# Retention in pairs of tiles, with states made a pair ahead, in a kernel of retention, routed experts and a dense layer

## Chip, core and metric

The kernel runs on one core of a Trainium2 chip. The metric is the device time of one execution in microseconds. Engines are called TensorE (PE in the rows; PEld is its loading of stationary operands), VectorE (DVE), ScalarE (ACT), GpSimd (POOL) and SyncE (SP, which issues most of the DMAs).

## What is computed

```python
def _attn_ref(q, k, v):                      # (8, 8, 576, 64) each
    scores = 1 / sqrt(64) * (q @ k.T)
    gamma = 1.0 - 2.0 ** (-5.0 - arange(8))
    Dmat = where(rel >= 0, gamma[:, None, None] ** rel, 0.0)   # rel: distance of two positions
    return (scores * Dmat) @ v

def _moe_ref(x, w_gate, w1, w2):             # x (4608, 512), 8 experts of 1024
    logits = x @ w_gate
    expert_idx = argmax(logits, axis=1)
    gate_w = softmax(logits)[arange(N), expert_idx]
    for e in range(E):
        mask = expert_idx == e
        out[mask] = gate_w[mask, None] * (maximum(x[mask] @ w1[e], 0.0) @ w2[e])

def _moe2_ref(x, w_in, w_out):               # 512 -> 2048 -> 512
    return maximum(x @ w_in, 0.0) ** 2 @ w_out
```

The output is `_moe2_ref` of `_moe_ref` of the retention, in float32.

## The kernel before

**Retention** (lines 327 to 705) treats 36 tiles of 128 tokens with all eight heads. A sequence of 576 tokens has four chunks of 128 and one of 64; the fifth chunks of two sequences share a tile (`kind` gives sequence and chunk, chunk 4 being such a tile). Per tile `t`: `scores` multiplies keys and queries (64 rows of the array, both halves at once) into two PSUM banks, and VectorE multiplies them with a causal mask (line 393). `scale_v` scales the values on GpSimd. `out_x` adds two products in one bank: the inner one, of the state that earlier chunks left and the queries (line 435, or line 428 for chunk 4, where queries spread out with zeros in `zq` keep the two sequences apart), and the outer one, of values and masked scores (line 439, two 64-wide halves of the array). VectorE scales the result (447) and transposes it in blocks (451); every second tile SyncE writes the rows of two to `x_d` (`put`, four DMAs). `state` adds keys times values to an accumulator in PSUM (line 411), from which ScalarE copies the state for the next chunk (418).

**Routing** runs along. After two tiles, `logits` multiplies the pair with the gate weights (line 472; 32 columns of the array), ScalarE copies the result, and a `fold` one tile later transposes it (481) and VectorE sums it. When a group of eight (or six) tiles has its logits, `group` makes six steps of it: `one` (VectorE, the largest logit), `two` (matmuls that count, line 522 on, and four vector operations), `three` (ranks, lines 558 to 229), `first` of `route` (hit and b, 238 and 242), `second` (matmuls, 249) and `third` (253 or 255). One step is taken per tile. Behind the third group, `lead_rows` fetches two tiles of tokens for the first expert, and `lead_turn` transposes each of them into a bank of the scores' pool (ScalarE 603, VectorE 604).

**Order.** Each engine executes its instructions in the order in which the program is written; nothing reorders them. The loop over `t` (644 to 693) issues the load of tile t + 4, the writes of the last pair, scores of t + 1, values of t + 2, the fold, logits, `out_x` and `state` of t, and one routing step. Input tiles have five buffers (a tile is 1 MB), scores three PSUM banks, results two, the accumulator, the logits and the routing one each. Four expert units are loaded at tiles 12, 18, 24 and 30 (`load_unit`) and split into a high and a low part two tiles later by ScalarE and GpSimd (`split_unit`).

Behind the loop the **experts** begin with the lead tiles (`first(0, (0,))`, line 955, whose first matmul reads the high part of both and whose second reads the low part), among which the last fold, routing steps and logits stand; experts and the **dense layer** (line 1144 on) fill the rest.

Of the kernel before, what the change touches and what calls it, by code (L numbers as in the profile page):

```python
# [19 lines left out]
NT = 36  # L20
# [33 lines left out]
def body(ctx, tc, att, tab_v, tab_x, masks, wg, ident, pick, cst, wu, wd, out):  # L54
# [269 lines left out]
    rt = scope(chain, "rt", 1, side="right")  # L324
    lg_ps = scope(chain, "lg_ps", 1, PSUM, side="right")
    rt_ps = scope(chain, "rt_ps", 1, PSUM, side="right")
    with ExitStack() as es:
# [5 lines left out]
        r_p = scope(es, "r_p", 2)  # L333
        sc_ps = scope(es, "sc_ps", 3, PSUM)
        x_ps = scope(es, "x_ps", 2, PSUM)
# [7 lines left out]
        lgt = rt.tile([128, NT, NE], F32, name="lgt")  # L343
        zq = tabs.tile([128, 4, 3, 64], F32, name="zq")
        sts = [tabs.tile([128, 4, 128], F32, name=f"sts{i}") for i in range(4)]

        in_t, vs_t, r_t, st_acc, xp_t, xr_t = {}, {}, {}, {}, {}, {}
        lead_s = []
# [8 lines left out]
        def load(t):  # L357
# [5 lines left out]
            else:  # L363
                sp.dma_start(out=a[:, 0:n], in_=att[t, :, 0:n])

        def spread_q(t):
            if kind(t)[1] == 4:
                q = in_t[t][:, 0].rearrange("p (h n) -> p h n", h=4)
                act.activation(out=zq[:, :, 0], in_=q[:, :, 0:64], func=AF.Copy)
                act.activation(out=zq[:, :, 2], in_=q[:, :, 64:128], func=AF.Copy)  # L370

# [47 lines left out]

        def out_x(t):  # L420
            b, c = kind(t)
            q = in_t[t][:, 0].rearrange("p (h n) -> p h n", h=4)
            ps = x_ps.tile([128, 4, 128], F32, tag="x", name="x")
            if c == 4:
                for i in range(2):
                    s = stslot(i, 3)
                    for p in range(4):
                        pe.matmul(
                            ps[:, p], s[:, p], zq[:, p, i:i + 2].rearrange("p a n -> p (a n)"),
                            start=(p == 0 and i == 0), stop=False, skip_group_check=True,  # L430
                        )
            elif c > 0:
                s = stslot(b, c - 1)
                for p in range(4):
                    pe.matmul(ps[:, p], s[:, p], q[:, p], start=(p == 0), stop=False, skip_group_check=True)  # L435
# [15 lines left out]
            vec.transpose(  # L451
                out=xr[:, 4 * (t % 2):4 * (t % 2) + 4].rearrange("q t k j -> q k t j"),
                in_=x.rearrange("q k (t i) -> q k t i", i=32),
            )
            if t % 2 == 0:
                return

            def put():
                rows = x_d[128 * t - 128:128 * t + 128, :].rearrange("(t i) (a c) -> a i t c", i=32, a=4)
                for a in range(4):  # L460
                    sp.dma_start(
                        out=rows[a], in_=xr[32 * a:32 * a + 32].rearrange("q t k j -> q t (k j)")
                    )

            late.append(put)

        def logits(j):
            x = xp_t.pop(j)
            both = lg_ps.tile([128, 2, 256], F32, tag="lg", name="lg")
            ps = both[:, 0]  # L470
# [18 lines left out]

        total = [None]  # L490

        def group(t0, t1):
# [143 lines left out]
        for a in sts:  # L636
            vec.memset(a, 0.0)
        vec.memset(zq, 0.0)
        vec.memset(wg2, 0.0)
        scale_v(0)  # L640
        scores(0)
        scale_v(1)
        fold = None
        for t in range(NT):
            ready, late[:] = late[:], []
            if t + 4 < NT:
                load(t + 4)
            if t == 0:
                sp.dma_start(out=wg2[:, :, 0:NE], in_=wg)
            if t == 2:  # L650
                sp.dma_start(out=idn, in_=ident)
            if t == 4:
# [4 lines left out]
            if t % 6 == 0 and 12 <= t < 36:  # L657
                raw[t] = load_unit(t // 6 - 2)
            if t + 1 < NT:
                scores(t + 1)  # L660
            if t + 2 < NT:
                scale_v(t + 2)
            if t == 1:
                vec.reciprocal(out=step, in_=tabx[:, 0, :, 0])
                vec.tensor_tensor(out=step, in0=step, in1=tabx[:, 1, :, 0], op=ALU.mult)
            if t in (1, 2):
                pool.tensor_tensor(
                    out=tabx[:, t + 1], in0=tabx[:, t], in1=step.unsqueeze(2).to_broadcast([128, 4, 128]), op=ALU.mult
                )
            if t == 4:  # L670
                for s in range(2):
# [3 lines left out]
                    )  # L675
            if fold:
                fold()
                for g in GROUPS:
                    if g[1] == t - 2:
                        todo += group(*g)  # L680
            fold = logits((t - 3) // 2) if t % 2 and t > 2 else None
            out_x(t)
            state(t)
            if t + 1 < NT:
                spread_q(t + 1)
            if NT - 1 - LEAD <= t < NT - 1:
                lead_turn(t - NT + 1 + LEAD)
            if todo and t < NT - 1:
                todo.pop(0)()
            if t == 8:  # L690
                vec.tensor_copy(ub, cf[:, C_U:C_U + 128])
            if t % 6 == 2 and 12 <= t < 36:
                split_unit(t // 6 - 2, raw.pop(t - 2), pool)()
        for f in late:
# [11 lines left out]


    xt_p = scope(ctx, "xt_p", 2, reuse="tile")
    HALF = CAP // 2
# [57 lines left out]
    with ExitStack() as es:  # L767
# [187 lines left out]
        first(0, (0,))  # L955
        fold()
        for f in todo:
# [565 lines left out]
```

## Time and profile before

| | us |
|---|---|
| median of 3 runs | 1352.97 (1352.24 to 1353.36) |
| the profiled execution | 1352.63 |
| its span | 1350.8 |
| TensorE busy | 1338.0 (99%) |
| VectorE, ScalarE, GpSimd busy | 835.2, 545.9, 256.6 |
| first expert matmul starts | 155.87 |

Busy time of TensorE counts a matmul from its start to its modelled end; several overlap, so it shows where TensorE had no work and not how fast it was. The retention is the first 155.87 us.

### The profile page before, as it was taken

How to read it: one execution, taken by the hardware profiler on the slowest of the kernel's cores; microseconds unless marked ns; L12 is line 12 of the kernel's file. 1: busy time of each engine (PE TensorE's matmuls, PEld its weight loads, DVE VectorE, ACT ScalarE, POOL GpSimd, SP SyncE). 2: the span in 40 equal slices, each digit the busy share in tenths (PEclk: the TensorE clock that was granted, in tenths of full speed). 3: DMA queues.
4: the chain of work that ended last, by engine and by line, in shares of the span. 5: the costliest groups of instructions: out<-in, count | busy, mean ns of one | idle time of the engine just before them, and what ended most of it. 6: DMA issues, size and time to landing. Idle time of an engine off the chain costs nothing.

```text
span 1350.8 us, 21535 instructions
## 1 busy us (share of the span) xinstructions
PE 1338.0 (99%) x8113; PEld 1152.5 (85%) x8113; DVE 835.2 (62%) x1512; ACT 545.9 (40%) x1064; POOL 256.6 (19%) x265
## 2 busy tenths in 40 slices
PE   8999999999999999999999999999999999999998
PEld 6888899999999999989888888888888888888887
DVE  6888858788788887636755563346624465245422
ACT  1232335445454553425544443345423454244321
POOL 3243263141332421112210030001300012000000
PEclk9999999999999999999999999999999999999999
DMA  9999678788978877567766666665766666565563
GB/s 341 344 350 323 175 225 291 256 299 262 299 256 255 301 257 268 202 243 269 284 232 203 208 218 233 216 223 195 251 210 225 212 221 235 201 215 194 190 230 110
DMA packets 129904, 328.32 MB, mean 243 GB/s; under 512 B 20350, under 2 KB 74110, under 8 KB 107776
## 3 DMA queue, kind: packets, MB, share of 16 engines
q1 hardware_dynamic: 121600, 305.72, 66.2%
q0 software_dynamic: 8192, 21.15, 5.3%
q8 instruction: 65, 1.06, 0.3%
q14 instruction: 47, 0.39, 0.1%
HBM read 266.10 MB, written 61.75 MB: 243 GB/s over the span
## 4 chain that ended last, share of the span: by engine, by line
PE 81%; issue 6%; DMA 6%; DVE 5%; ACT 2%; SPq 1%; POOL 0%; POOLq 0%; DVEq 0%; ACTq 0%
PE b L1187 25%; PE fa L1260 10%; PE fa L1259 10%; PE fa L1261 10%; PE l L830 3%; PE l L831 3%; PE l L832 3%; PE acc L854 3%; PE acc L855 3%; PE acc L856 3%; PE sc L387 2%; PE x L439 2%; PE x L435 1%; DMA in<-att 1%; PE stp L411 1%
## 5 line engine op out<-in xcount | busy, mean ns | idle before, releaser
L1187 PE MATMUL b<-xt,wq 128*128 128x512 f32 (+1 forms) x1296 | 265.2, 362 | 2.8 <-DMA wq<-ws_d 1.1
L1187 PEld LDWEIGHTS b<-xt,wq 128*128 128x128 f32 x1296 | 221.1, 188 | 41.9 <-DMA wq<-ws_d 1.5
L1259 PE MATMUL fa<-wq,ch 128*128 128x512 f32 x576 | 224.1, 389 | 0.0
L1260 PE MATMUL fa<-wq,ch 128*128 128x512 f32 x576 | 224.1, 389 | 0.0
L1261 PE MATMUL fa<-wq,cl 128*128 128x512 f32 x576 | 224.1, 389 | 0.0
L1249 DVE TENSOR_TENSOR cl<-g,ch 128x512 fp32r<-128x512 f32 (+1 forms) x160 | 108.6, 687 | 175.3 <-ACT ch L1248 172.9
L1248 ACT ACTIVATE ch<-g 128x512 fp32r<-128x512 f32 (+1 forms) x160 | 91.5, 584 | 183.5 <-PE fa L1260 183.5
L750 POOL TENSOR_TENSOR xsum<-yf 128x256 f32<-128x256 f32 x80 | 63.8, 805 | 452.8 <-DVE yf L738 389.1
L832 PE MATMUL l<-xt,w 128*128 128x320 f32 (+1 forms) x480 | 149.2, 311 | 0.0
L831 PE MATMUL l<-xt,w 128*128 128x320 f32 (+1 forms) x480 | 149.2, 311 | 0.0
L830 PE MATMUL l<-xt,w 128*128 128x320 f32 (+1 forms) x480 | 149.0, 310 | 0.1
L1261 PEld LDWEIGHTS fa<-wq,cl 128*128 128x128 f32 x576 | 108.1, 188 | 22.6 <-DVE cl L1249 0.2
L1259 PEld LDWEIGHTS fa<-wq,ch 128*128 128x128 f32 x576 | 108.1, 188 | 22.4
L1260 PEld LDWEIGHTS fa<-wq,ch 128*128 128x128 f32 x576 | 108.1, 188 | 22.4
L854 PE MATMUL acc<-w,hh 128*128 128x512 f32 x320 | 125.6, 393 | 0.1
L855 PE MATMUL acc<-w,hh 128*128 128x512 f32 x320 | 125.3, 392 | 0.0
L856 PE MATMUL acc<-w,hl 128*128 128x512 f32 x320 | 124.7, 390 | 0.0
L1173 ACT ACTIVATE s<-b 128x512 f32<-128x512 f32 (+1 forms) x120 | 66.5, 555 | 105.0 <-PE b L1187 105.0
L836 ACT ACTIVATE hh<-l 128x320 fp32r<-128x320 f32 (+2 forms) x128 | 54.4, 436 | 121.1 <-PE l L832 117.0
L1208 DVE TENSOR_TENSOR s<-s,s 128x512 f32<-128x512 f32 (+1 forms) x40 | 25.5, 638 | 113.7 <-ACT s L1173 113.7
L830 PEld LDWEIGHTS l<-xt,w 128*128 128x128 f32 x480 | 90.1, 188 | 2.6 <-DVE hl L837 0.4
L1187 PE MATMUL b<-xe,wq 128*128 128x512 f32 x384 | 92.2, 389 | 0.0
(181 smaller groups left out, 2082.0 us busy)
## 6 DMA issues: line engine op xcount, KB each, us to landing
wq<-ws_d SPq DMA_DIRECT2D x142, 1024.0 KB, 4.9
raw<-wu SPq DMA_DIRECT2D x62, 512.0 KB, 5.3
in<-att SPq DMA_DIRECT2D x28, 1024.0 KB, 8.1
craw<-wd SPq DMA_DIRECT2D x32, 512.0 KB, 5.2
ws_d<-cw SPq DMA_DIRECT2D x24, 512.0 KB, 4.4
x_d<-xr SPq DMA_DIRECT2D x72, 128.0 KB, 6.1
r_d<-row SPq DMA_DIRECT2D x35, 256.0 KB, 4.7
xs<-r_d SPq DMA_DIRECT2D x140, 64.0 KB, 4.4
```

Source lines behind the costliest of these rows:

```text
L830: pe.matmul(ps, w[:, 0, k], hi[:, k, cs], start=(k == 0), stop=False)
L831: pe.matmul(ps, w[:, 0, k], lo[:, k, cs], start=False, stop=False)
L832: pe.matmul(ps, w[:, 1, k], hi[:, k, cs], start=False, stop=(k == 3))
L854: pe.matmul(acc[i], hh[:, cs], w[:, 0], start=(f == 0), stop=False)
L855: pe.matmul(acc[i], hh[:, cs], w[:, 1], start=False, stop=False)
L856: pe.matmul(acc[i], hl[:, cs], w[:, 0], start=False, stop=(f == 7))
L1187: pe.matmul(ps, w[:, a, c], xc[T][i, b][c], start=(i in (5, 1, 4) and m == 0), stop=(m == 5), skip_group_check=True,)
L1248: act.activation(out=hi[:, o], in_=s, func=AF.Copy)
L1249: vec.tensor_tensor(out=lo[:, o], in0=s, in1=hi[:, o].bitcast(F32), op=ALU.subtract)
L1259: pe.matmul(acc[i], hi[:, cs], w[:, 0], start=(f == 0), stop=False)
L1260: pe.matmul(acc[i], hi[:, cs], w[:, 1], start=False, stop=False)
L1261: pe.matmul(acc[i], lo[:, cs], w[:, 0], start=False, stop=(f == 15))
```

## The change

The loop goes over pairs of tiles. In one pass it issues scores of both tiles, logits of the pair before, inner products of both, the fold, routing matmuls, and then for each tile its outer products, with the state of the second tile between them and the state of the next pair's first tile behind them. `out_x` falls into `inner` and `outer`. The transpose of a pair's second tile is issued in the next pass, behind the masks, with the writes that need it. Routing steps: at most one that begins with a matmul is taken per pass (the set `on_pe`), directly behind the fold, and then all up to the next such step. Scores have four banks, and the logits use one of them in turn; the logits' own bank is there only behind the loop. `zq` is gone: chunk 4's inner products take 64 query columns per sequence. Loads of t + 5 and t + 6 stand at the end of the pass; the gate weights and the identity are loaded in the first pass. Expert units are loaded from tile 24 on, one a pass, and split one pass later. The lead tiles are transposed at the end of the last two passes.

```diff
-        sc_ps = scope(es, "sc_ps", 3, PSUM)
+        sc_ps = scope(es, "sc_ps", 4, PSUM)
...
-        def out_x(t):
+        def inner(t):
...
                     for p in range(4):
+                        cs = slice(64 * i, 64 * i + 64)
                         pe.matmul(
-                            ps[:, p], s[:, p], zq[:, p, i:i + 2].rearrange("p a n -> p (a n)"),
+                            ps[:, p, cs], s[:, p], q[:, p, cs],
...
+        def outer(t):
+            b, c = kind(t)
+            ps = ps_t.pop(t)
...
-            late.append(put)
+            late.append(lambda: (spin(), put()))
...
-            both = lg_ps.tile([128, 2, 256], F32, tag="lg", name="lg")
+            if j < NT // 2 - 1:
+                both = sc_ps.tile([128, 4, 128], F32, tag="sc", name="lg").rearrange("p a b -> p (a b)")
...
+            on_pe.update((two, steps[4]))
...
-        for t in range(NT):
+        for t in range(0, NT, 2):
...
+            if t + 2 < NT:
+                scale_v(t + 2)
+            scores(t)
+            scores(t + 1)
             for f in ready:
                 f()
...
+            fold = logits(t // 2 - 1) if t else None
+            inner(t)
+            if t:
+                inner(t + 1)
+                fold()
+            if todo and todo[0] in on_pe:
+                todo.pop(0)()
+            for g in GROUPS:
+                if g[1] == t:
+                    todo += group(*g)
+            while todo and todo[0] not in on_pe:
+                todo.pop(0)()
+            outer(t)
+            if t == 0:
+                inner(1)
+            state(t + 1)
+            outer(t + 1)
+            if 2 < t + 2 < NT:
+                state(t + 2)
+            for u in (t + 5, t + 6):
+                if u < NT:
+                    load(u)
+            if t + 3 < NT:
+                scale_v(t + 3)
...
+            if t >= NT - 2 * LEAD:
+                lead_turn((t - NT) // 2 + LEAD)
+            if t == 24:
+                raw[0] = load_unit(0)
+            if 24 < t <= 32:
+                u = t // 2 - 13
+                split_unit(u, raw.pop(u), pool)()
+                if u < 3:
+                    raw[u + 1] = load_unit(u + 1)
```

TensorE, tiles 6 and 7 before: `sc` are scores, `lg<-x` logits, `lg<-idn` the fold, `x<-in` inner and `x<-r` outer products, `stp` states; of the outer products only the first row stands.

```order
L387 MATMUL sc<-in 128x128 x8
L472 MATMUL lg<-x,wg_144 32x256 x4
L435 MATMUL x<-in,sts_147 128x128 x4
L439 MATMUL x<-r_462,vs 64x128
...
L411 MATMUL stp<-vs,in 64x64 x8
L387 MATMUL sc<-in 128x128 x8
L481 MATMUL lg<-idn,ls 128x128 x2
```

The same engine after the change, a pass in which both tiles have an inner product:

```order
L379 MATMUL sc<-in 128x128 x16
L476 MATMUL lg<-x,wg_141 32x256 x4
L428 MATMUL x<-in,sts_144 128x128 x4
L428 MATMUL x<-in,sts_143 128x128 x4
L485 MATMUL lg<-idn,ls 128x128 x2
L436 MATMUL x<-r_507,vs 64x128
...
L403 MATMUL stp<-vs,in 64x64 x8
L436 MATMUL x<-r_521,vs 64x128
...
L403 MATMUL stp<-vs,in 64x64 x8
```

Stretches of one array shape have joined; each tile had scores, logits or fold, and 64-wide products apart.

VectorE, the second to fourth routing steps of the first group before (`r` are masked scores, `x<-x` the scaled result, `xr` its transpose):

```order
L393 TENSOR_TENSOR r_899<-sc,msk 128x512
L393 TENSOR_TENSOR r_901<-sc,msk 128x512
L447 TENSOR_TENSOR x<-x,tabx 128x4x128
L451 STREAM_TRANSPOSE xr<-x 128x4x4x32
L238 TENSOR_TENSOR hit<-cf,pl 128x40
L242 TENSOR_TENSOR b<-oh_99,hit 128x640
L393 TENSOR_TENSOR r_953<-sc,msk 128x512
```

After the change they stand in one pass, between the fold's sum and the first product:

```order
L486 TENSOR_REDUCE lgt<-lg 128x16
L535 TENSOR_SCALAR oh_99<-oh,cf 128x8x8
L536 TENSOR_TENSOR oh_99<-oh,cf 128x8x8
L549 TENSOR_REDUCE tf<-oh 128x8
L553 CAST tot<-tf 128x8
L562 TENSOR_TENSOR pr<-rkp,oh 128x64
...
L229 TENSOR_TENSOR a<-cf,pl 128x1024
L238 TENSOR_TENSOR hit<-cf,pl 128x40
L242 TENSOR_TENSOR b<-oh_99,hit 128x640
L444 TENSOR_TENSOR x<-x,tabx 128x4x128
```

Masks and products of three tiles no longer lie between these steps.

## Rows read from the trace of the kernel before

**Rows 1.** Ten microseconds: length, busy time (instructions) of five engines, PEclk, DMA share, GB/s.

```profile
30.00:40.00 10.00, 10.00 (x146) 8.49 (x140) 6.69 (x11) 2.29 (x6) 3.13 (x3) 1.00 1.02 358
```

**Rows 2.** Order of time, TensorE: start, length, engine, line, operation, form, count.

```profile
26.84 0.44 PE L481 MATMUL lg<-idn,ls 128*128 128x128 f32 x2
27.21 1.09 PE L439 MATMUL x<-r,vs 128*64 128x128 f32 x16
...
32.93 1.16 PE L387 MATMUL sc<-in 64*128 64x128 f32 x16
34.02 0.44 PE L481 MATMUL lg<-idn,ls 128*128 128x128 f32 x2
34.30 1.06 PE L435 MATMUL x<-in,sts 128*128 128x128 f32 x8
35.29 1.09 PE L439 MATMUL x<-r,vs 128*64 128x128 f32 x16
36.21 0.64 PE L411 MATMUL stp<-vs,in 128*64 128x64 f32 x16
36.77 1.16 PE L387 MATMUL sc<-in 64*128 64x128 f32 x16
...
38.44 1.16 PE L435 MATMUL x<-in,sts 128*128 128x128 f32 x8
...
41.01 0.49 PE L387 MATMUL sc<-in 64*128 64x128 f32 x4
```

**Rows 3.** Waits of TensorE, 10 to 152 us: total, times, longest.

```profile
PE rkp L249 <- DVE b L242: 0.7, 1, 0.7
PE rkp L522 <- DVE oh L514: 0.7, 1, 0.7
```

**Rows 4.** Order of time, ScalarE, behind the state of 36.21.

```profile
36.95 0.78 ACT L418 ACTIVATE sts<-stp 64x256 f32<-64x256 f32 x2 [3.13 <-PE stp L411]
```

**Rows 5.** Order of time, VectorE, in the first group's routing.

```profile
57.70 0.23 DVE L531 TENSOR_SCALAR oh<-oh,cf 128x64 bf16<-128x64 bf16 x1
...
58.34 1.28 DVE L393 TENSOR_TENSOR r<-sc,msk 128x512 f32<-128x512 f32 x2
...
60.41 0.69 DVE L447 TENSOR_TENSOR x<-x,tabx 128x512 f32<-128x512 f32 x1 [0.66 <-PE x L439]
...
61.77 0.18 DVE L558 TENSOR_TENSOR pr<-rkp,oh 128x64 f32<-128x64 f32 x1
...
63.67 1.28 DVE L393 TENSOR_TENSOR r<-sc,msk 128x512 f32<-128x512 f32 x2
```

**Rows 6.** Line 242 by itself: count, least/median/longest ns, first and last start.

```profile
L242 DVE TENSOR_TENSOR b<-oh,hit x5: 659/824/1594, 66.4 to 165.4; 128x640 bf16<-128x640 bf16 x3, 128x480 bf16<-128x480 bf16 x2
```

**Rows 7.** The lead tile's copies, in the same columns.

```profile
L603 ACT ACTIVATE lead<-turn x2: 597/597/597, 147.2 to 153.1; 128x512 fp32r<-128x512 f32 x2
L604 DVE TENSOR_TENSOR lead<-turn,lead x2: 653/672/691, 148.9 to 153.8; 128x512 fp32r<-128x512 f32 x2
```

**Rows 8.** DMA issues to 150 us: count, KB each, median us to landing.

```profile
in<-att SPq DMA_DIRECT2D x28, 1024.0 KB, 8.1
...
wg<-wg SPq DMA_DIRECT2D x1, 16.0 KB, 9.9
```

**Rows 9.** Stretches of the start, columns as in rows 1.

```profile
7.00:8.60 1.60, 0.00 (x0) 0.00 (x0) 1.21 (x2) 0.00 (x0) 1.04 (x1) 1.00 0.98 279
9.00:12.00 3.00, 3.00 (x30) 2.78 (x30) 1.29 (x2) 0.00 (x0) 0.00 (x0) 0.50 1.02 382
```

**Rows 10.** Loads of stationary operands, 20 to 150 us: count, busy us, mean ns, idle before.

```profile
L439 PEld LDWEIGHTS x<-r,vs 128*64 128x64 f32 x497 | 26.6, 136 | 5.2 <-issue 1.2 <-POOL vs L374 1.0
L435 PEld LDWEIGHTS x<-in,sts 128*128 128x128 f32 x176 | 21.3, 191 | 4.5 <-issue 3.7 <-ACT w L115 0.4 <-ACT sts L418 0.4
```

**Rows 11.** Order of time, SyncE's queue.

```profile
11.69 0.70 SPq L649 DMA_DIRECT2D wg<-wg  x1
...
42.13 3.06 SPq L461 DMA_DIRECT2D x_d<-xr  x4
```

More of the change, by code (lines that the diff above doesn't have):

```diff
@@ L324, in body @@
     rt = scope(chain, "rt", 1, side="right")
-    lg_ps = scope(chain, "lg_ps", 1, PSUM, side="right")
     rt_ps = scope(chain, "rt_ps", 1, PSUM, side="right")
@@ L343, in body @@
         lgt = rt.tile([128, NT, NE], F32, name="lgt")
-        zq = tabs.tile([128, 4, 3, 64], F32, name="zq")
         sts = [tabs.tile([128, 4, 128], F32, name=f"sts{i}") for i in range(4)]
-        in_t, vs_t, r_t, st_acc, xp_t, xr_t = {}, {}, {}, {}, {}, {}
+        in_t, vs_t, r_t, st_acc, xp_t, xr_t, ps_t = {}, {}, {}, {}, {}, {}, {}
         lead_s = []
@@ L364, in load @@
                 sp.dma_start(out=a[:, 0:n], in_=att[t, :, 0:n])
[L366 to L370, printed above, removed]
         def scale_v(t):
@@ L418, in state @@
                 act.activation(out=s[o, :, o], in_=acc[o], func=AF.Copy)
-        def out_x(t):
+        def inner(t):
             b, c = kind(t)
             q = in_t[t][:, 0].rearrange("p (h n) -> p h n", h=4)
-            ps = x_ps.tile([128, 4, 128], F32, tag="x", name="x")
+            ps = ps_t[t] = x_ps.tile([128, 4, 128], F32, tag="x", name="x")
             if c == 4:
@@ L450, in out_x, with spin @@
             xr = xr_t[t // 2]
[L451 to L454, printed above, removed]
+            def spin():
+                vec.transpose(
+                    out=xr[:, 4 * (t % 2):4 * (t % 2) + 4].rearrange("q t k j -> q k t j"),
+                    in_=x.rearrange("q k (t i) -> q k t i", i=32),
+                )
             if t % 2 == 0:
-                return
+                return spin()
             def put():
@@ L463, in put @@
                     )
-            late.append(put)
+            late.append(lambda: (spin(), put()))
         def logits(j):
             x = xp_t.pop(j)
-            both = lg_ps.tile([128, 2, 256], F32, tag="lg", name="lg")
+            if j < NT // 2 - 1:
+                both = sc_ps.tile([128, 4, 128], F32, tag="sc", name="lg").rearrange("p a b -> p (a b)")
+                both = both.rearrange("p (t n) -> p t n", t=2)
+            else:
+                both = lg_ps.tile([128, 2, 256], F32, tag="lg", name="lg")
             ps = both[:, 0]
@@ L488, in logits @@
             return fold
-        total = [None]
+        total, on_pe = [None], set()
         def group(t0, t1):
@@ L637, in body @@
             vec.memset(a, 0.0)
-        vec.memset(zq, 0.0)
         vec.memset(wg2, 0.0)
         scale_v(0)
-        scores(0)
         scale_v(1)
-        fold = None
-        for t in range(NT):
+        for t in range(0, NT, 2):
             ready, late[:] = late[:], []
-            if t + 4 < NT:
-                load(t + 4)
             if t == 0:
+                load(4)
                 sp.dma_start(out=wg2[:, :, 0:NE], in_=wg)
+                sp.dma_start(out=idn, in_=ident)
             if t == 2:
-                sp.dma_start(out=idn, in_=ident)
-            if t == 4:
@@ L653, in body @@
                 sp.dma_start(out=msk[:, 1], in_=masks[:, 1])
                 sp.dma_start(out=cf, in_=cst)
+            if t + 2 < NT:
+                scale_v(t + 2)
+            scores(t)
+            scores(t + 1)
             for f in ready:
                 f()
[L657 to L663, printed above, removed]
+            if t in (0, 2):
+                state(t)
@@ L664, in body @@
+            outer(t + 1)
[6 more added lines that the diff above has]
+                scale_v(t + 3)
+            if t == 0:
                 vec.reciprocal(out=step, in_=tabx[:, 0, :, 0])
                 vec.tensor_tensor(out=step, in0=step, in1=tabx[:, 1, :, 0], op=ALU.mult)
[L666 to L669, printed above, removed]
@@ L670, in body @@
-            if t == 4:
+                for c in (2, 3):
+                    pool.tensor_tensor(
+                        out=tabx[:, c], in0=tabx[:, c - 1], in1=step.unsqueeze(2).to_broadcast([128, 4, 128]),
+                        op=ALU.mult,
+                    )
+            if t == 2:
                 for s in range(2):
@@ L675, in body @@
                     )
[L676 to L690, printed above, removed]
-                vec.tensor_copy(ub, cf[:, C_U:C_U + 128])
-            if t % 6 == 2 and 12 <= t < 36:
-                split_unit(t // 6 - 2, raw.pop(t - 2), pool)()
+            if t == 6:
+                vec.tensor_copy(ub, cf[:, C_U:C_U + 128])
+            if t >= NT - 2 * LEAD:
[7 more added lines that the diff above has]
+                    raw[u + 1] = load_unit(u + 1)
         for f in late:
@@ L705, in body @@
                 sp.dma_start(out=halves[v][s], in_=wu[v, :, 512 * s:512 * s + 512])
+    lg_ps = scope(chain, "lg_ps", 1, PSUM, side="right", reuse="tile")
     xt_p = scope(ctx, "xt_p", 2, reuse="tile")
@@ L955, in body @@
         first(0, (0,))
-        fold()
         for f in todo:
```

## The prediction

> **What bounds the kernel now.** I read the page first (TensorE busy 1338.0 of 1350.8 us, in the table above), then ten-microsecond stretches of the part that changes, then its instructions in order of time, and last what waits for whom. In the retention part TensorE has no idle time, VectorE is busy for two thirds and the DMA engines all the time [rows 1]. The order in time says what "busy" means: a pair of tiles takes 41.01 - 32.93 = 8.08 us, stretch after stretch of matmuls of one array shape, with no gap between them [rows 2]. Between 10 and 152 us TensorE waited for VectorE only twice, 0.7 us each, in the routing [rows 3]. After the retention the experts and the second layer keep TensorE just as full. So what the loop gains or loses on TensorE up to the first expert's matmuls passes to the end one for one; only order, shapes and new waits on TensorE count.
>
> **What a change of shape costs.** Two comparisons give it. From start to next start, the fold's transposes take 27.21 - 26.84 = 0.37 us where outer products of another shape follow, and 34.30 - 34.02 = 0.28 where inner products of the same shape follow: leaving a shape costs 0.09. The eight inner instructions last 1.06 us behind the fold and 1.16 behind the logits: entering costs 0.10 [rows 2]. So 0.19 a change. A change into the 64-wide shape is cheaper: the outer products, which enter but don't leave (the states follow in their shape), take 36.21 - 35.29 = 0.92, where as many score matmuls, entering and leaving, take 1.09; 0.09 of that is leaving, so entering is some 0.08 cheaper. I take 0.12 for these.
>
> **The change part by part.**
>
> *Two tiles at a time.* In the order of TensorE's instructions I count 128 stretches of one shape before the first expert matmul, and 75 after the change: 18 instead of 35 of scores, 20 instead of 36 of the 64-wide shape, 20 instead of 40 of the full one. Of the 53, three fall into the start, which is counted below. The other 50 are 35 at 0.19 and 15 at 0.12: 8.4 us gained. With every change at 0.12 it would be 6.0, at 0.19 9.5.
>
> *Routing steps behind the fold.* They run in the fold's shape (counted above), and their inputs come from the pair before, so the two waits of 0.7 go [rows 3]: 1.4 us gained, nothing at worst.
>
> *States one pair ahead.* The state of tile t+2 follows the outer products of t+1 and adds to the bank that ScalarE has still to copy for t+1. Today the state's matmuls start at 36.21 and end at 36.85 [rows 2], and the two copies run from 36.95 to 37.73 [rows 4]. In the new order TensorE would be through with the state at 36.21 + 0.57 and with the outer products 0.92 later, at 37.70; the copies end at 37.73 and the hand-over costs the 0.10 seen between 36.85 and 36.95. A wait of 0.13, 14 times: 1.8 us lost, between 0 and 3.
>
> *Routing steps on VectorE, in one pair instead of three tiles.* A plain pair costs VectorE two times 1.28 for masks, two times 61.77 - 60.41 = 1.36 for a product and its transpose, and some 0.2 for the fold's reduction (as the 0.18 at 61.77): 5.5 us [rows 5]. TensorE's pair will be 8.08 less three changes of shape plus 0.13, about 7.7; 2.2 us of VectorE are free. Now the second step (58.34 - 57.70 = 0.64), the third (63.67 - 61.77 = 1.90) and the product b (0.82, [rows 6]) stand in one row, ahead of the pair's products: 3.4 us, 1.2 too many. Nothing hides this: the next pair's logits need the last product, and their bank is the one that the first scores of that pair used, so they wait for its mask as well, and TensorE executes in order. That is 1.2 us for each group of eight tiles, 0.6 more for the third (four more small operations, each like the 0.18 at 61.77), 0.9 for the group of six: 1.2 + 1.2 + 1.8 + 0.9 = 5.1. The third group's matmul on the total stands right behind its step and waits for 0.64 + 0.2 of VectorE: 0.8. The first transposed lead tile holds a bank that the next scores want until VectorE, late by then, has taken it: one operation of 0.67 [rows 7]. Together 6.6 us lost. The lower end is 2 (the backlog fades before the logits); the upper is 10, since b has also taken 1.59 [rows 6], and then the same overrun grows by 0.8 a group. I add 1.2 for that: half of the groups with some of it, because VectorE's products will now stand where GpSimd is scaling the next values.
>
> *Lead transposes.* The second one was followed by a whole tile; now it stands right before the first expert matmul, which needs its high part (ScalarE, 0.60) and, one matmul later, its low part (VectorE, 0.67) [rows 7]. With three hand-overs of 0.1 less the 0.1 of a matmul, 1.5 us that nothing covers; 0.6 at the least.
>
> *The start.* The first logits move from behind scores of tile 4 to before them, and wait for the gate weights. These are issued behind tile 4's load, as now, and land 9.9 us after an issue at 11.7 [rows 8, 11], at 21.6. At that time the old order has the inner and outer products of tile 2 done (1.1 + 0.9, [rows 2]) and the new one has not: 2.1 us lost, 1 at the least. It can be more: today TensorE is idle from 7 to 8.6 us, and from 9 to 12 the granted clock is 0.50, the 1.2 GHz level [rows 9]. A second such fall in the wait for the weights would add 1.5 us, half of those 3.
>
> *Plain inner products for the fifth chunks.* Sixteen instructions of 128 columns become sixteen of 64. I cost this at nothing: loading 128 stationary columns takes 191 ns and 64 take 136 [rows 10], 0.86 ns for each column more, so 110 ns for 128, and the instructions already follow each other at (35.29 - 34.30 - 0.09) / 8 = 0.11 us [rows 2]. The load is the limit, and it stays. The Trainium skill, page "TensorE: Matmul & The Clock Gate", section "Back-to-back issue gap", lets the gap follow the streamed columns, which speaks for a gain here; its section "LDWEIGHTS (loading the stationary operand)" has the load follow the stationary's columns, which agrees with the rows. The first reading is a rival below.
>
> *Loads and units.* The same bytes and the same number of transfers. Expert units move to tiles 24 to 32, whose copies ScalarE (2.3 of 10 us, [rows 1]) and GpSimd have room for: nothing on the path.
>
> **Sum.** -8.4 - 1.4 + 1.8 + 6.6 + 1.2 + 1.5 + 2.1 = +3.4 us. The profiled execution took 1352.6, the median of the runs is 1353.0, so 0.3 above: 1352.6 + 3.4 + 0.3, about 1356.4.
>
> **Rivals.**
>
> *The backlog fades: faster.* If VectorE's overrun is taken up by the free time of the next pair before the logits ask, 6.6 + 1.2 go: 1348.6. For it: VectorE is a third idle. Against it: its free time lies between products and masks, behind the backlog. It decides at an overrun under 0, that is at routing steps of 2.2 us in a pair.
>
> *Loads come late: slower still.* Loads of t+5 and t+6 are issued behind four writes of rows, and these behind a transpose that now follows four masks: 1.1 us for the first scores, two times 1.28 for masks and 0.6 for the transpose, so 4.3 us into the pair, plus 3.1 for issuing the writes [rows 11]: 7.4. Landing takes 8.1 [rows 8], which makes 15.5, and scores of t+5 start two pairs later, at 2 x 7.7 + 1 = 16.4: 0.9 us of slack. Beyond 9.0 us of landing time each microsecond costs half of one a pair; at 9.7 it is 0.35 in each of 16 pairs: 5.6 us, 1362.
>
> *The inner products do follow their columns: no change.* Sixteen instructions at 0.06 (the states' pace: (36.77 - 36.21 - 0.09) / 8, [rows 2]) instead of 0.11, four times: 3.2 us less, 1353.2. This is what the page's rule on the gap, named above, would make of it.
>
> *The shapes give nothing back.* If the 0.19 is no cost of the change but time in which earlier matmuls end anyway, the 8.4 don't come: 1364.8. Against it: the fold's two rows differ in nothing but what follows.
>
> **How the numbers follow.** My forecast 0.50, the fading backlog 0.15, late loads 0.13, inner products by columns 0.14, no gain by shape 0.08. The forecast's own range, from its bounds, is 1353.4 to 1359.4. A measurement tells 0.2% (2.7 us) from no change: below 1350.3 or above 1355.7. Faster: nearly all of the first rival, 0.14. Same: the third rival, 0.18 of my own case and a little of the first, 0.33. Slower: 0.53. The range is 1349.0 to 1363.0; it leaves out half of the first rival, and the upper ends of the late loads and of the last one, 0.19.
>
> **What would show it.** Right: plain pairs of 7.6 to 7.8 us; logits of tiles 12, 20, 28 waiting for VectorE by 1 us and more; states waiting for ScalarE by 0.1 to 0.2; the first expert matmul waiting for the lead's copies by about 1 us; first logits at 21.6. Wrong: pairs of 8 us (shapes give nothing), logits without waits (the backlog fades), scores waiting for loads in every pair, or fifth chunks whose inner products take half as long.

## The result and the profile after

| | before | after |
|---|---|---|
| median, us | 1351.88 (6 runs, 1351.06 to 1353.36) | 1367.97 (6 runs, 1360.9 to 1370.61) |
| profiled execution, its span | 1352.63, 1350.8 | 1368.13, 1366.3 |
| first expert matmul starts | 155.87 | 171.18 |

The ratio is 1.011, with a 95% interval of 1.0097 to 1.0123: the change costs 16 us where the prediction had 3.4. The loss is in the retention: the first expert matmul comes 15.3 us later, the last matmul of the program 15.5 us later; as the prediction said, what the retention loses is not made up behind it.

The waits of TensorE in the part that changed, by total (who waits and for whom, total in us, times, longest), after:

```profile
PE lg L476 <- DVE r L385: 6.0, 4, 2.2
PE sc L379 <- DVE lead L609: 2.8, 1, 2.8
PE sc L379 <- DMA in<-att: 2.5, 1, 2.5
PE lg L476 <- DVE xr L450: 2.0, 1, 2.0
PE lg L485 <- ACT ls L480: 1.3, 1, 1.3
PE warm L624 <- DVE ones L620: 1.1, 1, 1.1
PE rkp L560 <- DVE tot L551: 0.8, 1, 0.8
PE l L849 <- ACT lead L608: 0.7, 1, 0.7
```

The two routing waits of [rows 3] are gone, as forecast, and the logits, the lead's bank, the total and the lead's copy wait, as forecast. The same view of the kernel before, for 0 to 156 us, has only these beside [rows 3]:

```profile
PE sc L387 <- DMA in<-att: 2.8, 3, 1.7
PE warm L619 <- DVE ones L615: 1.1, 1, 1.1
...
PE x L428 <- ACT zq L369: 0.2, 1, 0.2
```

What the prediction didn't have shows in the stretches of time (columns as in [rows 1], whose stretch stands first; PEclk is the third number from the right), after:

```profile
30.00:40.00 10.00, 9.96 (x159) 8.45 (x160) 7.22 (x14) 3.03 (x8) 3.27 (x4) 1.00 0.62 187
20.00:24.00 4.00, 2.05 (x28) 1.36 (x27) 2.35 (x4) 1.14 (x3) 3.71 (x4) 0.85 1.02 407
24.00:28.00 4.00, 4.00 (x42) 3.83 (x43) 0.23 (x1) 0.00 (x0) 0.00 (x0) 0.72 1.02 340
...
96.00:100.00 4.00, 2.91 (x20) 2.50 (x21) 3.44 (x6) 0.38 (x1) 0.00 (x0) 0.74 0.99 410
...
160.00:164.00 4.00, 3.66 (x25) 2.63 (x26) 3.39 (x6) 0.38 (x1) 0.76 (x1) 0.50 0.02 4
```

In the same stretches of the kernel before the granted clock is 1.00; it has one fall, at its start [rows 9]. In order of time, the matmuls around them (start, length, engine, line, operation, form, count, and in brackets the idle time before and who ended it), after:

```profile
22.45 0.80 PE L476 MATMUL lg<-x,wg 128*32 128x256 f32 x8 [1.95 <-DVE xr L450]
23.18 3.48 PE L428 MATMUL x<-in,sts 128*128 128x128 f32 x16
...
69.21 2.06 PE L379 MATMUL sc<-in 64*128 64x128 f32 x32
71.19 0.64 PE L476 MATMUL lg<-x,wg 128*32 128x256 f32 x8
71.76 2.05 PE L428 MATMUL x<-in,sts 128*128 128x128 f32 x16
73.65 0.38 PE L485 MATMUL lg<-idn,ls 128*128 128x128 f32 x2
73.96 1.09 PE L436 MATMUL x<-r,vs 128*64 128x128 f32 x16
74.88 0.64 PE L403 MATMUL stp<-vs,in 128*64 128x64 f32 x16
75.35 1.05 PE L436 MATMUL x<-r,vs 128*64 128x128 f32 x16
76.50 0.69 PE L403 MATMUL stp<-vs,in 128*64 128x64 f32 x16
77.12 2.06 PE L379 MATMUL sc<-in 64*128 64x128 f32 x32
...
97.09 0.64 PE L476 MATMUL lg<-x,wg 128*32 128x256 f32 x8 [2.20 <-DVE r L385]
97.66 3.60 PE L428 MATMUL x<-in,sts 128*128 128x128 f32 x16
...
160.34 2.08 PE L379 MATMUL sc<-in 64*128 64x128 f32 x14 [2.83 <-DVE lead L609]
162.34 1.08 PE L476 MATMUL lg<-x,wg 128*32 128x256 f32 x8
```

Sixteen inner products last 2.05 us in the plain pair at 71.76, and 3.48 and 3.60 right behind stops of 1.95 and 2.20. These stops were paid twice: while TensorE stood still, and again while it worked at the granted clock of 0.50, the 1.2 GHz level. So was the stop of 2.83 before 160.34; another of 1.90, before 63.88, was not. The pair itself (69.21 to 77.12) is 7.91 us long, against 8.08 before [rows 2].

That splits the way to the first expert matmul into three parts. Idle is that time less TensorE's busy time. Low clock is worked out from stretches of 2 us: busy time in each, times one less its granted clock. The rest is work at full clock. By the rows above this counts a little too much as low clock (1.74 of the 3.48 us, where 1.43 were lost), and so too little as work.

| us | first expert matmul | idle | low clock | work |
|---|---|---|---|---|
| before | 155.9 | 5.7 | 1.5 | 148.6 |
| after | 171.2 | 19.2 | 9.1 | 142.9 |
| difference | +15.3 | +13.5 | +7.6 | -5.7 |
| predicted | +3.4 | +10.0 | 0 | -6.6 |

The last row sums the prediction's terms: work -8.4 + 1.8; idle -1.4 + 6.6 + 1.2 + 1.5 + 2.1. The size of the low-clock part differs from execution to execution: six of the changed kernel had spans of 1359.1 to 1368.8 us at mean clocks of 0.998 to 0.991. A difference of 0.007 in 1366 us is 9.6 us, about what the six times lie apart. The kernel before is not free of this: its six times here lie 2 us apart, but those taken beside the experiments 4 to 10 us, at clocks of 0.994 to 1.000.

### The profile page after: what moved, and what is told of

Same layout as the page of the kernel before. It is cut to its first block, busy times and chain, and to the rows that moved or that the text cites. A ratio compares the mean times of both kernels' runs of the same rounds, so it can differ in the third digit from the quotient of the medians.

```text
span 1366.3 us, 21551 instructions
## 1 busy us (share of the span) xinstructions
PE 1339.6 (98%) x8113; PEld 1154.5 (84%) x8113; DVE 835.9 (61%) x1511; ACT 542.8 (40%) x1056; POOL 258.8 (19%) x265
## 4 chain that ended last, share of the span: by engine, by line
PE 78%; DMA 7%; issue 6%; DVE 4%; SPq 2%; ACT 1%; POOL 1%; POOLq 0%; DVEq 0%; ACTq 0%
PE b L1205 24%; PE fa L1279 9%; PE fa L1277 9%; PE fa L1278 9%; PE l L850 4%; PE l L851 4%; PE l L849 4%; PE acc L873 3%; PE acc L874 3%; PE acc L875 3%; DMA in<-att 3%; DMA raw<-wu 2%; PE x L428 1%; PE x L436 1%; DMA r_d<-row 1%
## 5 line engine op out<-in xcount | busy, mean ns | idle before, releaser
L1226 DVE TENSOR_TENSOR s<-s,s 128x512 f32<-128x512 f32 (+1 forms) x40 | 25.5, 638 | 113.3 <-ACT s L1191 113.3
```

## The experiments

Theory 1: the change loses by stops of TensorE, nearly all for VectorE, and by the low clock behind them, while its pairs are shorter. Theory 2: the pairs are no better, or VectorE is the bound, so that a wait removed in one place returns in the next.

### What a stop costs, in the kernel before

ScalarE repeats its two copies of the state at six plain places; the kernel is the one before, else unchanged.

```diff
-            for h in range(2):
+            for h in range(2 + (8 if t in (5, 10, 15, 20, 24, 29) else 0)):
+                h %= 2
```

> The kernel before, with a stop of TensorE put in at six plain places: ScalarE repeats its two copies of the state four more times at tiles 5, 10, 15, 20, 24 and 29, so that the next inner products wait. Four times 0.78 us less the slack of 0.4 to 0.7 makes 2.4 to 2.7 us of standing still at each place. If a stop costs its own length and no more: 6 x 2.55 = 15 us, 1368. Theory 1 (behind a stop of this length TensorE runs at half clock for a while, which cost 1.6 to 1.7 us behind the stops at 22 and 97 us of the changed kernel): 6 x (2.55 + 1.7) = 25 us, 1378, with rows of granted clock 0.50 behind the six places; between the two if it falls behind some of them only.

> The same with two more pairs of copies instead of four: stops of 0.85 to 1.15 us at the same six places. Both theories: six times about 1.0, 1358.5, if no low clock follows a stop as short as this (none followed the one of 1.4 us at the logits of tile 28 in the changed kernel). If the clock falls behind short stops too: 1365 to 1369.

(In the second kernel 8 is 4.) Long stops: 1376.4 us, ratio 1.0172 (1.0155 to 1.0189), 23 us more. Short ones: 1359.5, ratio 1.0047 (1.003 to 1.0063), 6.2 more. The six long stops sum to 15.5 us and the six short ones to 5.8, so the short ones cost about themselves and the long ones 7.5 us over that; in the profiled execution with the long ones the first expert matmul comes 25.5 us later, with 16.0 us more idle. Stretches of 2 us around the first long stop:

```profile
36.00:38.00 2.00, 0.11 (x1) 0.11 (x1) 0.32 (x2) 1.74 (x5) 0.00 (x0) 0.97 0.96 279
38.00:40.00 2.00, 2.00 (x10) 1.78 (x12) 0.00 (x0) 0.00 (x0) 0.00 (x0) 0.50 0.97 365
40.00:42.00 2.00, 2.00 (x32) 1.98 (x32) 0.29 (x1) 0.00 (x0) 0.00 (x0) 0.67 0.72 222
42.00:44.00 2.00, 2.00 (x32) 1.42 (x27) 1.87 (x4) 0.91 (x3) 1.04 (x1) 1.00 0.43 85
```

TensorE stands still, then works at 0.50, and is back at 1.00 four us later. By order of time, the inner products behind the first and the fifth stop:

```profile
37.89 2.07 PE L436 MATMUL x<-in,sts 128*128 128x128 f32 x8 [2.65 <-ACT sts L419]
...
131.84 1.16 PE L436 MATMUL x<-in,sts 128*128 128x128 f32 x8 [2.51 <-ACT sts L419]
```

Low clock followed five of the six long stops, 1.6 to 3.0 us behind each and 11 in all by the counting above; behind the fifth, and behind all six short ones, there is none. So theory 1's second half is shown, with nothing of the change in the program: six stops of some 2.6 us cost about one and a half times their length (23 us for 15.5), because most of them, not all, were followed by the lower clock. The Trainium skill, page "TensorE: Matmul & The Clock Gate", section "HAM oscillation — how this bites in real kernels", describes a kernel that pays for each of its waits, about 3 to 5 us long, again in work at the throttled clock. These rows agree that a wait is paid again (2.65 us of standing still, then eight products in 2.07 instead of 1.16 us), but the stops here are shorter, and one of six was not followed by it.

### Each place by itself, in the changed kernel

First, the routing steps spread: one vector-only step per pass instead of all in a row.

```diff
-            while todo and todo[0] not in on_pe:
+            if todo and todo[0] not in on_pe:
```

> The changed kernel with at most one vector-only routing step per pass, so that count and ranks stand in one pass and hit and b in the next. Theory 1: 1.9 us less of VectorE in the crowded pass, so the waits of 1.9, 2.2 and 1.4 us at the logits of tiles 12, 20 and 28 shrink to 0.5 or less (4 us), the low clock behind the second goes (1.7 us), and in the last passes the steps of the fourth group come one pass later, with the wait of 2.8 us for the lead's bank shorter by as much: 1358 to 1362. Theory 2 (the waits come from VectorE's total work and not from where the steps stand): 1366 to 1368.

1362.4 us, ratio 1.007 (1.0053 to 1.0086). The four waits of the logits fell from 6.0 to 2.3 us, so they come in large part from where the steps stand. The wait for the lead's bank fell from 2.8 to 0.3 us, as expected, but one of 2.2 for the lead's low part came up at the second expert matmul, as theory 2 would have it. This kernel also had a wait that nobody forecast:

```profile
137.14 0.69 PE L485 MATMUL lg<-idn,ls 128*128 128x128 f32 x2 [2.67 <-ACT ls L480]
```

ScalarE, which executes in order, stood at the copy of an expert unit that had not landed, and the fold's input was queued behind it.

Second, the lead transposes, both moved into the last pass behind the fold.

```diff
-            if t >= NT - 2 * LEAD:
-                lead_turn((t - NT) // 2 + LEAD)
...
+            if t == NT - 2:
+                for i in range(LEAD):
+                    lead_turn(i)
             outer(t)
```

> The changed kernel with both transposes of the lead tiles moved into the last pass, behind the fold, where no scores follow in their banks. The wait of 2.8 us of the scores of tile 35 for a bank and the 0.7 + 0.3 us before the first experts go. Theory 1: VectorE's backlog (3.4 us of routing steps and 1.9 us of products ahead of the masks of tile 34) is still there, so the logits take over about 2 us of the wait and the low clock from 160 to 167 us stays in part: 1364 to 1366. Rival (the bank alone sets the end of the loop): wait and low clock go, 6 us and more, 1361.

1361.0 us, ratio 1.0063 (1.0045 to 1.0082): the rival's time, but not for its reason. The logits did take over the wait, as theory 1 said (2.74 us, for the mask of tile 34), and idle to the first expert matmul is 18.7 us against 19.2. What differs between the two traces is the clock: 3.2 us lost to it instead of 9.1, with 1.00 behind the stop of 2.74. Whether the move made the clock hold isn't shown: this execution was the fastest of four, whose mean clocks of 0.995 to 0.997 lie within the 0.991 to 0.998 of the changed kernel, and at 0.997 this kernel took 1359.4 us and the changed one 1364.6. How much of the 7 us is the clock stays open.

Third, the inner products ahead of the logits, in all passes and in the second alone.

```diff
-            fold = logits(t // 2 - 1) if t else None
             inner(t)
             if t:
                 inner(t + 1)
+                fold = logits(t // 2 - 1)
                 fold()
```

> The changed kernel with the inner products of both tiles issued ahead of the pair's logits instead of behind them; nothing else differs. Theory 1 (TensorE stands still for VectorE in the logits, and works at a lower clock after the longer of these stops): the 1.9 us of inner products now lie in the wait, so the four waits for masks (6.0 us) shrink to about 1.5, the one of 2.0 at 22 us goes, and with it most of the low clock at 23 to 27 and 97 to 101 us (1.6 and 1.7 us); the logits get two changes of shape of their own, some 1.7 us in all. About 1360. Theory 2 (VectorE is the bound of these passes, and a wait taken away at the logits comes back at the next place): the waits move to the inner products or the next scores, 1365 to 1368.

> The changed kernel with the same exchange in the second pass alone (tiles 2 and 3). Theory 1: the wait of 2.0 us at 22 us and the half clock behind it (16 inner products in 3.3 instead of 1.9 us) go, the rest stays: about 1364.5. If the start loses only because its loads land late, nothing is won: 1368. If the clock at 23 to 27 us falls for the stretch at half clock before it and not for the wait, about 2 us are won: 1366.

In all passes: 1370.8 us, ratio 1.0134 (1.0117 to 1.0151), where about 1360 was expected. The logits' waits did shrink, from 6.0 to 0.8 us, but 2.4 us of waits for VectorE came up at the inner products, as theory 2 has it; work grew from 142.9 to 146.1 us, and little low clock was left (1.5 us in the profiled execution, the fastest of four). But one wait was put in everywhere:

```profile
PE lg L485 <- ACT ls L480: 9.5, 17, 1.2
```

With nothing between logits and fold, the fold waits 0.5 us and more for ScalarE's copy, 17 times over. The expectation had not reckoned with this wait, and it is larger than what the logits gave back, so the time doesn't decide between the theories. In the second pass alone: 1365.6, ratio 1.0088 (1.0071 to 1.0105). Its trace has neither the stop nor the low clock at 22 to 27 us, but 14.2 us of low clock elsewhere; since the changed kernel's own times lie 10 us apart, the time decides nothing there.

### The fifth chunks

In the kernel before, only the change's plain inner products for chunk 4:

```diff
-                            ps[:, p], s[:, p], zq[:, p, i:i + 2].rearrange("p a n -> p (a n)"),
+                            ps[:, p, cs], s[:, p], q[:, p, cs],
```

> The kernel before, with the change's plain inner products for the fifth chunks alone: sixteen matmuls of 64 query columns instead of 128, and no spreading of the queries by ScalarE. If the load of the stationary operand sets the pace: the same within 1 us (in the changed kernel's trace the sixteen take 1.83 us from first to next start at full clock, before 1.99). If they followed their columns: 4 x 0.8 = 3.2 us faster, 1349.

1351.7 us, ratio 0.9979 (0.9962 to 0.9995): a gain of 0.7 to 5 us, where the forecast had none. The matmuls put it near the lower end. Sixteen of the 64-column matmuls take 45.86 - 44.04 = 1.82 us:

```profile
44.04 1.90 PE L429 MATMUL x<-in,sts 128*128 128x64 f32 x16
45.86 1.09 PE L440 MATMUL x<-r,vs 128*64 128x128 f32 x16
```

Before they took 1.99; four tiles make 0.7 us, and the wait of 0.2 for `zq` goes. At the states' pace of 0.06 they would take 1.0. The profiled execution, the slowest of ten (1355.5 us), shows the gain in its matmuls alone: it waited 6.2 us for loads of tiles, against 2.8 before, and 2.2 for a routing step. Behind that stop of 2.2 us its clock stayed at 1.00.

### All remedies together

The logits stand between the two inner products, steps are spread, the lead moved as above, the gate weights issued ahead of the rest of tile 1, the expert units loaded at tiles 12, 18, 24 and 30 again.

```diff
-            fold = logits(t // 2 - 1) if t else None
             inner(t)
             if t:
+                fold = logits(t // 2 - 1)
                 inner(t + 1)
                 fold()
```

> The changed kernel with all remedies: the logits between the two inner products (0.9 us of work ahead of them against the wait for the mask, 0.9 behind them against the wait of the fold for ScalarE's copy, which cost 17 times 0.6 when the logits stood behind both), one vector-only routing step per pass, both lead transposes in the last pass behind the fold, the gate weights issued ahead of the rest of tile 1, and the expert units loaded at the old tiles. Theory 1 (waits and the low clock behind them, 18 and 9 us of the first 171, are what the change lost; 15 of the 27 lie at places treated here): first expert matmul at 148 to 153 us instead of 171, time 1346 to 1351. Theory 2 (the pairs themselves are no shorter than the old order, the remedies only bring back the old time): 1352 to 1356.

1353.6 us, ratio 1.0005 (0.9996 to 1.0015): the whole loss is recovered, and no more. By its time alone that is theory 2's forecast (1352 to 1356), not theory 1's (1346 to 1351); the table below shows what each part came to. From there, logits in between in the four passes that need it only, and a group's total (the block from `if t1 < NT` on in `two`) moved to the end of `one`:

```diff
+            full = t in (2, 12, 20, 28)
+            fold = logits(t // 2 - 1) if t and not full else None
             inner(t)
             if t:
+                if full:
+                    fold = logits(t // 2 - 1)
                 inner(t + 1)
                 fold()
...
```

> The kernel with all remedies, in which the logits now stand between the inner products only in the four passes that need it (tiles 2, 12, 20, 28) and ahead of both in the others, as in the changed kernel; and the running total of a group is summed in its first routing step instead of its second. The logits in between cost 0.2 us more a pass (8.16 against 7.96 for tiles 16 and 17, 7.23 against 7.12 for 24 and 25): 13 passes, 2.6 us back; the wait of 0.8 us for the total and three of the four waits of 0.5 us of the fold go, and the low clock at 118 us that followed them in that run. Theory 1: 4 us faster than with the logits in between everywhere, 1348 to 1351. If the pairs' waits return at the logits of the other passes: 1353 or more.

From that kernel, the state of a pair's first tile in its own pass:

```diff
-            if t in (0, 2):
-                state(t)
+            state(t)
...
-            if 2 < t + 2 < NT:
-                state(t + 2)
```

> The previous kernel with the state of a pair's first tile made in its own pass, behind the scores, and not a pair ahead. Gone is the wait for ScalarE's copy (outer products to the next state 1.15 instead of 0.92 us, 14 times: 3.2 us). Back comes a stretch of 64-wide products of its own in each pass, one change of shape, 0.1 to 0.2 us times 16: 2.4 us. So about the same, within 1.5 us. If the state ahead only costs: 3 us faster. If it hides the copies from the inner products: slower by 2 us and more.

And, also from the kernel with the logits mixed, the expert units late again, as in the change:

```diff
-            if t in (12, 18, 24, 30):
-                raw[t // 6 - 2] = load_unit(t // 6 - 2)
+            if t == 24:
+                raw[0] = load_unit(0)
...
```

> The first kernel of this call with the expert units loaded from tile 24 on, one a pass, as in the change. If late units cost nothing (the forecast): the same within 1 us. If ScalarE, which executes in order, is held by the copy of a unit that has not landed and the fold then waits for ScalarE (1.3 us at 152 us in the changed kernel's trace, 2.7 us at 137 us with the steps spread): 1.5 to 4 us slower, more where the clock falls behind such a wait.

| us | time | ratio to before | first expert matmul | idle | low clock | work |
|---|---|---|---|---|---|---|
| all remedies | 1353.6 | 1.0005 (0.9996 to 1.0015) | 155.8 | 9.1 | 2.9 | 143.8 |
| logits mixed | 1352.1 | 0.9998 (0.9987 to 1.0008) | 152.5 | 8.4 | 1.6 | 142.5 |
| no state ahead | 1350.6 | 0.999 (0.9977 to 1.0003) | 151.7 | 9.4 | 0 | 142.2 |
| units late | 1353.6 | 1.0004 (0.9995 to 1.0014) | 156.0 | 12.2 | 1.4 | 142.4 |

All four have the change's work, 142 to 144 us against 148.6 before, so the part of theory 2 that has the pairs no better falls: the work is 5 to 6 us shorter, wherever the waits go. The split of the clock can't make this: without any low clock, "no state ahead" has 142.2 us of work, and the kernel before with the plain fifth chunks 147.9. But theory 2's other part holds: 3 to 6 us went into idle time that the kernel before doesn't have, and not all that is won at the first expert matmul reaches the end. With the logits mixed it comes 3.4 us earlier and the span is 1.4 us shorter; behind it TensorE waits 1.0 us for the lead's copy and 1.6 for VectorE's part of the experts' hidden values, where the kernel before has neither wait. Its time, 1352.1, missed the 1348 to 1351 that theory 1 expected. Late units cost 3.8 us of idle in these two traces; in time 1.5, which the intervals don't tell apart. The state ahead is worth nothing that the intervals show, as expected. The last kernel makes small moves on top of "no state ahead", all meant to shorten waits that its trace still had: the lead transposes ahead of the last routing steps, `load_rest(1)` ahead of the gate weights, and the two products into `oh2` in `one`.

```diff
+        load_rest(1)
         sp.dma_start(out=wg2[:, :, 0:NE], in_=wg)
         sp.dma_start(out=idn, in_=ident)
-        load_rest(1)
```

> The kernel with the states in their own pass, and four small moves: the lead transposes ahead of the last routing steps instead of behind them (the first expert matmul waited 1.0 us for VectorE, which had the steps first); the two products that only need a group's choice in its first step instead of its second (0.44 us of VectorE in each crowded pass, where the logits still waited 1.3 and 1.0 us); the gate weights behind the rest of tile 1 instead of ahead (a state waited 2.0 us for the second tile's values at 15 us, which GpSimd scales once they have landed). Theory 1 (what shortens a wait of TensorE in the loop shortens the whole): 2 to 3 us faster than without them, 1347 to 1349, 0.3% under the kernel before. If the waits only change place: 1350 to 1351.

1352.2 us, ratio 0.9999 (0.9987 to 1.0011). The wait for the lead went, but that of 2.0 us at the start only fell to 1.7, behind a new one of 1.0 for the load, and stops at the logits of 1.15 and 1.30 us stayed, the second with a clock of 0.50 from 118 to 120 us behind it. The waits changed place, as theory 2 has it, and the time is above what either theory expected (1347 to 1349, 1350 to 1351). No version is clearly faster than the kernel before.

## Why the prediction was wrong

**The bound, and one for one.** Right: +15.3 us at the first expert matmul became +15.5 at the end. The experiments show its limit, with 3.4 us won there and 1.4 kept.

**Shapes (-8.4).** Right in size. By the rows of the plain pair, scores of two tiles save 2 x 1.09 - 1.98 = 0.20, inner products with their fold 0.28 + 0.99 + 1.09 - 2.20 = 0.16, states 0.56 - 0.47 = 0.09: 0.45 in a pair, where 0.50 was forecast. The plain pair came to 7.91 us, a little over the 7.6 to 7.8 that was forecast, because the next term took more back. The rival that shapes give nothing is out, by 141 to 146 us of work in every kernel with pairs.

**States ahead (+1.8).** Right mechanism, low price: 76.50 - 75.35 = 1.15 from the outer products to the state, against 0.92, so 0.23 instead of 0.13, 14 times 3.2 us, just over the upper bound of 3. With this term and the shapes, work came out at -5.7 for -6.6.

**Routing steps in one pass (+7.8 with the share of b).** Right mechanism, and the places named: logits of tiles 12, 20 and 28 wait 1.90, 2.20 and 1.37 us, with 0.52 at tile 18, and the total 0.82. VectorE ahead of the stop at 97.09 (columns as above), after:

```profile
91.47 1.23 DVE L229 TENSOR_TENSOR a<-cf,pl 128x1024 bf16<-128x1024 f32 x1
92.61 1.04 DVE L238 TENSOR_TENSOR hit<-cf,pl 128x40 bf16<-128x40 f32 x1
93.69 0.82 DVE L242 TENSOR_TENSOR b<-oh,hit 128x640 bf16<-128x640 bf16 x1
94.43 0.68 DVE L444 TENSOR_TENSOR x<-x,tabx 128x512 f32<-128x512 f32 x1
95.15 0.71 DVE L450 STREAM_TRANSPOSE xr<-x 128x512 f32<-128x512 f32 x1
95.78 0.65 DVE L444 TENSOR_TENSOR x<-x,tabx 128x512 f32<-128x512 f32 x1
96.36 2.47 DVE L385 TENSOR_TENSOR r<-sc,msk 128x512 f32<-128x512 f32 x4
```

No gap: the steps push the products, these push the mask, and the logits start 0.1 us behind the first mask's end. The share of b was right in kind: b lasted 1.60 in the first group, against 0.82 and 0.83 in the next two, and `hit`, above, 1.04, against 0.19 in these others. `hit` ends at 93.65, with GpSimd's scaling of values:

```profile
92.14 1.45 POOL L366 TENSOR_TENSOR vs<-in,tabv 128x512 f32<-128x512 f32 x1 [4.86 <-DMA in<-att]
```

No run takes GpSimd's work away, so that this is the cause is read from the times alone. The term that was mis-sized is the lead's bank: the prediction took one operation of 0.67, but that operation stands behind the fourth group's steps and two products on VectorE, and the scores of tile 35 waited 2.83. All of it makes 9.6 for 7.8. VectorE and GpSimd ahead of that wait, after:

```profile
152.40 0.23 DVE L486 TENSOR_REDUCE lgt<-lg 128x16 f32<-128x64 f32 x1 [2.07 <-PE lg L485]
152.54 1.32 DVE L535 TENSOR_SCALAR oh<-oh,cf 128x48 bf16<-128x48 bf16 x1
...
151.47 2.36 POOL L117 TENSOR_TENSOR w<-raw,w 128x1024 fp32r<-128x1024 f32 x1 [3.72 <-ACT w L115]
```

VectorE had stood idle for 2.07 us, because the fold was late (units, below); then the first step lasted 1.32 us, where the other groups' last 0.23, and ended with GpSimd's split of a unit at 153.8. So the late units are part of this wait too; how much of it is not shown.

**The start (+2.1).** Right size, other releaser: the logits waited 1.95 us until 22.45, for the transpose that now stands behind four masks (in the kernel with the lead moved they waited 3.0 for the gate weights, until 21.06). The low clock behind it is the one fall that the prediction saw, as 1.5 us that could come on top of its sum.

**Lead copies (+1.5).** 0.7 and 0.3. **Units (nothing).** Wrong: the fold waited 1.26 us at 152 us for ScalarE, held by a unit that had not landed. With these, idle is +13.5 for +10.0.

**The step that failed** is the sum's silence on the clock in the loop. The prediction read [rows 9], where the granted clock is 0.50 behind an idle stretch of 1.6 us, and used it for the start alone, as 1.5 us that its sum leaves out; the stops of 1.2 us and more that it forecast for each group were counted once. Of the 12 us missed, 6.2 are low clock in the loop: 1.6 behind the stop at 22 us, 1.7 behind the one at 97 and 2.9 behind the one at 160. Another 1.4 are more low clock at 8 to 16 us, ahead of all these stops; the other traces have 0 to 1.6 us of it there, so that the change is the cause isn't shown. 3.5 are idle, of which 2.2 the lead's bank, and 0.9 work. The one execution of the change at a mean clock of 0.998 took 1360.9 us, inside the stated range.

The range ended at 1363, because no rival had the low clock as its mechanism. It was narrow by the prediction's own terms too: their upper bounds (-6.0, 0, 3, 10, and 1.5 and 2.1 where none is given) add up to +10.6, or 1363.6, and 1365.1 with the 1.5 for the clock, where it called 1359.4 the end of its forecast's own range.

**Rivals.** The backlog did not fade. Loads of tiles were not late: behind the start no scores waited for one. The inner products don't follow their columns: 0.114 us apart for 64 and 0.124 for 128. The rule that the gap follows the streamed columns, of the Trainium skill's page "TensorE: Matmul & The Clock Gate", section "Back-to-back issue gap", decides little here: the same section has a stream of loads and matmuls spaced by both, and the load of 128 stationary columns is the same for both forms. The section "LDWEIGHTS (loading the stationary operand)", by which the load follows the stationary columns, agrees with [rows 10].

## What to carry to other kernels

When a change puts a wait on TensorE, look for the granted clock behind waits in the same trace, and price each wait with and without the slower work behind it; a range that leaves this out is too short on one side. A gain from fewer changes of shape is real and can be read from starts of matmuls, but it needs the other engines' work spread as evenly as it was: here some 6 us of work were won and 21 lost to waits and low clock, and no later kernel got the 6 us into its time. Where an engine executes in order, follow what stands behind a wait on it: one late transfer in ScalarE's queue stopped a transpose that had nothing to do with it.

## What the runs showed of the hardware that was not expected

Whether the clock falls behind a stop isn't settled by its length. Of stops between 2.45 and 2.71 us in the kernel before, five of six were followed by 0.50. The stop at the logits of tile 12 lasted 1.90 us in the changed kernel and 1.97 with the lead moved, with no fall behind either, and 1.98 with the start exchanged, with 0.57 from 60 to 64 us. With the lead moved, stops of 2.97 and 2.74 us were followed by none and one of 2.21 was. Six stops of 0.83 to 1.09 us were followed by none, but one of 1.30 in the last kernel was (0.50 from 118 us, 3 us behind its end), and 0.56 and 0.81 us close together, at 117 and 118 us with all remedies, were followed by 0.55. What else decides it stays open.
